# Two-level Strassen-Winograd products: the vector engine's sums in pieces between PSUM readings, the attention products ahead of long products, and q turned at the head of the stage

## The chip, the cores and the metric

The kernel runs on one core of one Trainium2 chip. The metric is the device time of one execution in microseconds. The kernel before was timed three times: 1026.94, 1013.04 and 1013.72 us, median 1013.72 us. The trace below is of a further execution, which took 1017.5 us.

## The reference

All data are float32 (the two weight matrices reach the kernel as 64-bit words, which it folds into float32 first).

```
kv  = einsum('bhsd,bhse->bhde', k, v)          # 8 batches, 8 heads, 576 x 64
o   = einsum('bhsd,bhde->bhse', q, kv)
x   = o / sqrt(mean(o*o, -1) + 1e-6) * g_norm  # then (4608, 512)
h   = x @ w_in                                 # 512 -> 2048
g   = s * max(h, 0)**2 + b
out = g @ w_out                                # 2048 -> 512
```

## The kernel before, in words

The 4608 rows are cut into 36 chunks of 128, and four chunks make a unit: nine units, u = 0 to 8. A unit has two stages. The first is x @ w_in with relu and square, by one level of the Strassen-Winograd scheme (seven products instead of eight, paid for with additions): for each of four blocks `s` of the hidden width the steps x1, z2, x6, y7, x5, x3, y4. It leaves g in SBUF as tiles a11, a12, a21, a22 and their sum s1. The second stage is g @ w_out, again by seven products. In units 2 to 8 the products 2, 7 and 4 use the scheme a second time, on quarters: `second_level` (L677) gives for each of them, called p2, p7 and p4 here, a step `sums` and seven small products in the order 1, 2, 6, 7, 5, 3, 4. Each small product is four 128x128x128 matrix products on TensorE, which the trace shows as eight MATMULs. A long product (x1, x6, x5, x3 for j = 0 and 1) has eight 128x128x256 ones, sixteen MATMULs.

`sums` makes four tiles of 128x512 on VectorE: s1 = x21 + x22 (needed by small product 5), s2 = s1 - x11 (product 6), s3 = x11 - x21 (product 7), s4 = x12 - s2 (product 3). Small products 1, 6, 5 and 3 accumulate into the same PSUM bank, and between them VectorE must read the bank: `keep` (L697 and on) takes product 1 out as r1 before product 6 may add to it, takes r2 out before product 5, and r4 before product 3. Product 2 has a bank of its own, and 7 and 4 share one. So TensorE can run ahead of a reading by only one small product.

Also on VectorE, in the second stage: the sums S2 (`s2`, four subtractions in place on a11, used by x6) and S4 (`s4`, four on a12, used by x3); and the work for the next unit's attention, chunk c = 0 to 3 of it. For each chunk `turn` transposes q in 32x32 blocks (VectorE, L391), `product` multiplies with kv on TensorE (L421, 32 MATMULs of 128 columns) into one single bank, ScalarE squares it (L430), VectorE reduces (L432), ScalarE takes the root (L436), VectorE inverts and scales (L438, L440, which frees the bank), and `turn_x` transposes the result (L464); after every second chunk ScalarE multiplies by g_norm (L470). `x_sums` (L484) then forms the four sums of the next x.

The order is written by hand: every engine runs its instructions in the order in which the program text issues them. `mm2(u)` (L646) returns 14 slots, and `side_of(u)` (L1039) gives the attention steps that follow slot n. The loop at the end runs slot, then side. Between slot 0 and slot 1 stand the last two steps (x3, y4) of the first stage. `pump(2)` lets SyncE (SP) issue the loads of the next two blocks of w_out into a ring of seven; `loads(u)` issues the q loads at the start of a unit.

In the second stage before, p2's `sums` and the reading of x1(1) come first, then all of S2, then p2's small products; S4 stands ahead of p7's small products in the same way; turn c+1 follows one slot after product c; and an attention product follows a long product.

Of the kernel before, what the change touches and what calls it, by code (L numbers as in the profile page):

```python
# [15 lines left out]
def kernel(  # L16
# [211 lines left out]
    def add(o, a, b):  # L228
        nc.vector.tensor_tensor(out=o, in0=a, in1=b, op=ALU.add)  # L229

    def sub(o, a, b):
        nc.vector.tensor_tensor(out=o, in0=a, in1=b, op=ALU.subtract)  # L232
# [410 lines left out]
    out_18 = out.rearrange("(b t j) n -> b j t n", t=32, j=JC)  # L643
    G_OF = {1: "a11", 2: "a12", 3: "a12", 4: "a22", 5: "s1", 6: "a11", 7: "a21"}

    def mm2(u):  # L646
        st = {}

        def product(i, j, ps, first):
# [27 lines left out]
        def second_level(i, other, to):  # L677


            a, t, r = {}, {}, {}  # L680
            cols = [slice(q * P, q * P + P) for q in range(2)]

            def quarter(j, h):
                g = g_pair[G_OF[i], h].rearrange("p s b t -> p (s b) t")
                return g[:, :, j * P : j * P + P]

            def sums():
                x11, x12, x21, x22 = (quarter(j, h) for j in range(2) for h in range(2))
                s1, s2, s3, s4 = (
                    late["sub"].tile([P, FC // 4, P], FP32, name="sub", tag="sub")  # L690
                    for _ in range(4)
                )
                add(s1, x21, x22)
                sub(s2, s1, x11)
                sub(s3, x11, x21)
                sub(s4, x12, s2)
                a.update({1: x11, 2: x12, 3: s4, 4: x22, 5: s1, 6: s2, 7: s3})  # L697

            def go(m, bank, first):
                if first:  # L700
                    t[bank] = bank_of((bank, i), "z" if bank == "z" else "y", 1 if bank == "z" else 2)
                    t[bank] = t[bank].rearrange("p b n -> p (b n)")[:, :P]
                n = ORDER.index(m)
                w = ring[u, i, n // 2][:, n % 2]
                for f in range(FC // 4):
                    matmul(t[bank], a[m][:, f], w[:, f], first and f == 0, f == FC // 4 - 1)

            def keep(name, j, q):
                r[name] = late["tmp"].tile([P, P], FP32, name="r", tag="r")
                scaled(r[name], t["x"], other(j, cols[q]))  # L710

            def m1():
                go(1, "x", True)
                keep("r1", 0, 0)

            def m2():
                go(2, "z", True)
                scaled(to(0, cols[0]), t["z"], r["r1"])

            def m6():  # L720
                go(6, "x", False)
                keep("r2", 1, 0)

            def m7():
                go(7, "y", True)

            def m5():
                go(5, "x", False)
                keep("r4", 1, 1)
                scaled(to(1, cols[1]), t["y"], r["r4"])  # L730

            def m3():
                go(3, "x", False)
                scaled(to(0, cols[1]), t["x"], other(0, cols[1]))

            def m4():
                go(4, "y", False)
                scaled(to(1, cols[0]), t["y"], r["r2"])

            return {"sums": sums, 1: m1, 2: m2, 6: m6, 7: m7, 5: m5, 3: m3, 4: m4}  # L740
# [26 lines left out]
        def x1(j):  # L767
            st["x", j] = half(("x", j), "x")
            product(1, j, st["x", j], True)
            if u > 0:  # L770
                part("r1", j, st["x", j], b1)
# [20 lines left out]
            else:  # L792
                scaled(rows("o1", j)[:, :HN], ps, st["r1", j])

        def s2():
            for s in range(NS):
                sub(ga["a11", s], ga["s1", s], ga["a11", s])

        def s4():
            for s in range(NS):  # L800
                sub(ga["a12", s], ga["a12", s], ga["a11", s])

        def x6(j):
# [31 lines left out]
        def seq(fn, *more):  # L835
            def run():
                fn()
                for m in more:
                    m()
            return run  # L840
# [52 lines left out]
        def x6_of(j):  # L893
            product(6, j, st["x", j], False)
            part("r2", j, st["x", j], b_12)
# [16 lines left out]
            else:  # L912
                store("o2", j, 4 * u + 2 + j)

        def run(steps, *which):
            for m in which:
                steps[m]()

        return [
            lambda: x1(0),  # L920
            seq(p2["sums"], lambda: x1(1), lambda: pump(2), s2),
            seq(lambda: run(p2, 1, 2, 6, 7), lambda: pump(2)),
            seq(p2[5], lambda: x6_of(0)),
            seq(lambda: run(p2, 3, 4), lambda: pump(2), p7["sums"]),
            seq(lambda: x6_of(1), lambda: pump(2), s4),
            seq(lambda: run(p7, 1, 2, 6, 7), lambda: pump(2)),
            seq(p7[5], lambda: x5_of(0)),
            seq(p7[3], lambda: with_7(0), p7[4], lambda: pump(2)),
            seq(lambda: x5_of(1), lambda: with_7(1), lambda: pump(2), p4["sums"]),
            lambda: x3(0),  # L930
            seq(lambda: run(p4, 1, 2, 6, 7, 5), lambda: pump(2)),
            seq(lambda: x3(1), lambda: pump(2)),
            seq(lambda: y4_of(0, 3), lambda: y4_of(1, 4), lambda: pump(2)),
        ]


    NU = FC // 2
# [101 lines left out]
    def side_of(u):  # L1039

        if u + 1 >= U:
            return {}
        turn, product, norm, turn_x, _ = zip(*(attention(c) for c in range(4 * u + 4, 4 * u + 8)))
        product = [whole(*steps) for steps in zip(product, norm)]
        side = {
            2: [turn[0]],
            3: [product[0]],
            4: [turn[1]],
            5: [turn_x[0], product[1]],
            6: [turn[2]],  # L1050
            7: [turn_x[1], product[2]],
            8: [turn[3]],
            9: [turn_x[2], product[3]],
            11: [turn_x[3]],
            12: [lambda: [sums() for sums in x_sums(u + 1)]],
        }
        if u == 0:
            side = {
                6: [lambda: kv_product(1)],
                7: [turn[0]],  # L1060
                8: [product[0], turn[1]],
                9: [turn_x[0], product[1], turn[2]],
                10: [turn_x[1], product[2], turn[3]],
                11: [turn_x[2], product[3]],
                12: [turn_x[3], lambda: [sums() for sums in sums_w_in(0)]],
                13: side[12],
            }
        return side
# [24 lines left out]
    for u in range(U):  # L1093
        if u > 0:
            loads(u)
        steps = [mm1(u, s) for s in range(NS)] if u > 0 else []
        slots = []
        for s, a in enumerate(steps):
            slots.append(a["x1"])
            if s:  # L1100
                slots.append(steps[s - 1]["x3"])
            slots.append(a["z2"])
            if s:
                slots.append(steps[s - 1]["y4"])
            slots += [a["x6"], a["y7"], a["x5"]]
        if u == 0:
            first_unit()
        for n, slot in enumerate(slots):
            slot()
            if u == 1 and n in (1, 3, 5):  # L1110
                for sums in sums_w_in((n + 1) // 2):
                    sums()
            if u in kv_due and n == 12:
                kv_product(kv_due[u])
            elif u + 1 in kv_due and n == 14:
                for i in range(2):
                    load_kv(kv_due[u + 1], i, late["kv"], tag="kv")
        second, side = mm2(u), side_of(u)
        for n, slot in enumerate(second):
            slot()  # L1120
            if u == 0:
                if n == 1:
                    for i in range(2):
                        load_kv(1, i, convp, tag="raw", bufs=3)
                    store_w2(1)
                    loads(0)
                    store_w2(5)
                elif n == 2:
                    t2 = convp.tile([P, 4 * R * D], FP32, name="w_t2", tag="raw", bufs=3)
                    W2_AT[6] = t2[:, : FC // 2 * HN].rearrange("p (f n) -> p f n", n=HN)  # L1130
                    for i in range(14, 16):
                        more(i)
                    sub_w_out(6, 3, 5)
                    store_w2(3, 2, 6)
            if n == 0 and u > 0:
                for step in ("x3", "y4"):
                    steps[-1][step]()
            for step in side.get(n, []):
                step()
        if u == 0:  # L1140
            tc_late()
            for i in range(2):
                load_kv(kv_due[1], i, late["kv"], tag="kv")
            pump(7)
# [30 lines left out]
```

## Time and profile before

| | us |
|---|---|
| the profiled execution, its own time | 1017.5 |
| its span, first to last instruction | 1015.7 |
| TensorE (PE) busy | 959.4 |
| VectorE (DVE) busy | 580.0 |
| ScalarE (ACT) busy | 194.8 |
| mean granted TensorE clock | 0.987 |
| unit 3, first stage (358.30 to 405.65 us of the span) | 47.35 |
| unit 3, second stage (405.65 to 467.56) | 61.91 |

The engine table says that TensorE is busy nearly throughout. So the view to read is that of TensorE's idle time and of who ended it, and then the order of time of TensorE and VectorE through one second stage. A row of the view in order of time has the start, the length, the engine, the line, the instruction with what it writes and reads, and how often it stands in a row; in brackets is the idle time before it and who released it. Time is in microseconds from the start of the span.

### The profile page before, as it was taken

Reading aid. Unit: us, or ns where it says so; the run is one execution under the profiler, and the core shown is the slowest. Engines: PE = TensorE matmul, PEld = TensorE weight load, DVE = VectorE, ACT = ScalarE, POOL = GpSimd, SP = SyncE. Lnnn points to the kernel's source line nnn. Section 1 sums busy time; section 2 is a strip of 40 time slices with the busy share of each in tenths; the row PEclk is TensorE's granted clock in tenths of the full one; section 3 lists DMA queues with packets and bytes.
Section 4 is the critical chain, followed back from the end, with each engine's and each line's share of the span. In section 5 each row is a group of like instructions: output and inputs, shape, how many; then the busy total and the mean of one; then the engine's idle time right before and its main releaser. Section 6 shows DMA issues by size and latency. Waiting matters only on the chain. (4 is left out here: it accounts for less than half of the span.)

```text
span 1015.7 us, 16743 instructions
## 1 busy us (share of the span) xinstructions
PE 959.4 (94%) x6934; PEld 847.5 (83%) x6934; DVE 580.0 (57%) x1019; ACT 194.8 (19%) x366; POOL 6.7 (1%) x18
## 2 busy tenths in 40 slices
PE   7999999999997999889988999799988998899987
PEld 7888888888886988779877888688877988798877
DVE  2798775564456544674465644654457455564553
ACT  3672122111210112011201121012201110112100
POOL 2000000000000000000000000000000000000000
PEclk9999999999999999999999999999999999999999
DMA  9689646687345454356164634546025522452053
GB/s 251 218 291 255 209 113 200 143 271 216 57 110 159 135 147 104 95 175 171 26 159 135 196 72 104 160 126 162 14 85 184 168 32 65 133 164 65 16 181 93
DMA packets 127531, 143.71 MB, mean 141 GB/s; under 512 B 76256, under 2 KB 87264, under 8 KB 127328
## 3 DMA queue, kind: packets, MB, share of 16 engines
q1 hardware_dynamic: 124352, 140.88, 48.6%
q10 hardware_dynamic: 2784, 1.77, 0.8%
q8 instruction: 54, 0.88, 0.4%
q14 instruction: 21, 0.17, 0.1%
q0 software_dynamic: 320, 0.00, 0.0%
HBM read 120.33 MB, written 22.28 MB: 140 GB/s over the span
## 5 line engine op out<-in xcount | busy, mean ns | idle before, releaser
L90 PE MATMUL x_ps<-w_sb,a 128*128 128x256 f32 x768 | 175.1, 382 | 0.0
L90 PEld LDWEIGHTS x_ps<-w_sb,a 128*128 128x128 f32 x768 | 144.5, 191 | 20.1 <-issue 1.6
L90 PE MATMUL y_ps<-w_sb,sub 128*128 128x128 f32 x672 | 95.6, 302 | 36.7 <-DVE r L659 36.7
L90 PEld LDWEIGHTS y_ps<-w_sb,sub 128*128 128x128 f32 x672 | 89.2, 213 | 42.5 <-DVE r L659 39.3
L90 PE MATMUL y_ps<-xs,wb 128*128 128x256 f32 x512 | 121.0, 379 | 0.0
L90 PE MATMUL x_ps<-xs,ws 128*128 128x256 f32 x512 | 121.0, 379 | 0.0
L229 DVE TENSOR_TENSOR a<-y_ps,r 128x512 f32<-128x512 f32 x64 | 44.0, 688 | 122.2 <-ACT r L568 122.2
L568 ACT COPY r<-x_ps 128x512 f32<-128x512 f32 x96 | 56.3, 586 | 284.2 <-PE x_ps L90 277.5
L90 PEld LDWEIGHTS x_ps<-xs,ws 128*128 128x128 f32 x512 | 97.3, 190 | 13.2
L90 PEld LDWEIGHTS y_ps<-xs,wb 128*128 128x128 f32 x512 | 97.3, 190 | 13.2
L90 PE MATMUL x_ps<-xT,wa 128*128 128x256 f32 x384 | 89.6, 380 | 0.1
L90 PEld LDWEIGHTS x_ps<-xT,wa 128*128 128x128 f32 x384 | 72.4, 190 | 10.2 <-ACT xT L470 0.5
L523 DVE SCALAR_TENSOR_TENSOR a<-a 128x512 f32<-128x512 f32 x96 | 66.5, 692 | 3.3
L601 DVE TENSOR_TENSOR a<-a 128x512 f32<-128x512 f32 x32 | 22.1, 692 | 75.9 <-ACT a L600 75.9
L90 PE MATMUL y_ps<-w_sb,a 128*128 128x128 f32 (+1 forms) x416 | 62.8, 297 | 0.0
L90 PE MATMUL x_ps<-xT,ws 128*128 128x256 f32 x256 | 61.1, 382 | 0.0
L90 PEld LDWEIGHTS y_ps<-w_sb,a 128*128 128x128 f32 x416 | 57.1, 191 | 4.1 <-issue 1.4
L90 PE MATMUL z_ps<-xT,wa 128*128 128x256 f32 x256 | 60.5, 379 | 0.0
L430 ACT ACTIVATE xn<-x_ps 128x512 f32<-128x512 f32 x34 | 20.3, 597 | 204.3 <-PE x_ps L421 202.9
L90 PE MATMUL x_ps<-w_sb,s 128*128 128x256 f32 x256 | 57.8, 380 | 0.0
L90 PEld LDWEIGHTS z_ps<-xT,wa 128*128 128x128 f32 x256 | 48.7, 190 | 6.6
L90 PEld LDWEIGHTS x_ps<-xT,ws 128*128 128x128 f32 x256 | 48.2, 190 | 6.7
(122 smaller groups left out, 990.3 us busy)
## 6 DMA issues: line engine op xcount, KB each, us to landing
w_sb<-w SPq DMA_DIRECT2D x133, 512.0 KB, 4.4
kv_sb<-in_k_dram SPq DMA_DIRECT2D x30, 288.0 KB, 4.8
kv_sb<-in_v_dram SPq DMA_DIRECT2D x30, 288.0 KB, 7.1
w_raw<-in_moe_w_in_dram SPq DMA_DIRECT2D x8, 1024.0 KB, 7.8
w_raw<-in_moe_w_out_dram SPq DMA_DIRECT2D x8, 1024.0 KB, 5.2
out_dram<-o SPq DMA_DIRECT2D x104, 64.0 KB, 1.7
w_sb<-w SPq DMA_DIRECT2D x21, 256.0 KB, 2.8
q_sb<-in_q_dram SPq DMA_DIRECT2D x144, 32.0 KB, 2.1
```

What stands on the lines that cost most here:

```text
L90: nc.tensor.matmul(o, lhsT=lhsT, rhs=rhs, start=start, stop=stop, skip_group_check=True)
L229: nc.vector.tensor_tensor(out=o, in0=a, in1=b, op=ALU.add)
L430: nc.scalar.activation(st["xn"], st["x"], AF.Square)
L523: nc.vector.scalar_tensor_tensor(t, t, 0.0, t, ALU.max, ALU.mult)
L568: nc.scalar.copy(st[name], src)
L601: nc.vector.tensor_mul(t, t, t)
```

## The change

Units 2 to 8 get a second stage that is written out as one sequence, `first` and `second`, in place of the 14 slots. Four things move; no instruction is added or taken away on any engine.

- `sums` takes a list. p2's s1 and s2 are made ahead of the reading of x1(1), s3 and s4 each between two readings of p2's small products. p7's and p4's sums stay whole, and stand ahead of x6(0) and x3(0).
- S2 is made in two pieces, after small product 6 and after small product 5 of p2; S4 in four pieces among p7's small products.
- turn 0 and turn 1 stand at the head of the stage, ahead of x1(0); turn 2 and turn 3 after the attention steps 1 and 2.
- An attention product with its norm (`attend`) now stands ahead of the long products x6(0), x6(1), x5(0), x5(1), and `x_sums` ahead of x3(1).

The last unit has no attention for a next one, and so only the first two. Units 0 and 1 are as before.

```diff
-            def sums():
+            def sums(which=(5, 6, 7, 3)):
...
+                for m in which:
+                    a[m] = late["sub"].tile([P, FC // 4, P], FP32, name="sub", tag="sub")
...
-        def s2():
-            for s in range(NS):
+        def s2(steps=range(NS)):
+            for s in steps:
...
-            seq(p2["sums"], lambda: x1(1), lambda: pump(2), s2),
-            seq(lambda: run(p2, 1, 2, 6, 7), lambda: pump(2)),
-            seq(p2[5], lambda: x6_of(0)),
-            seq(lambda: run(p2, 3, 4), lambda: pump(2), p7["sums"]),
-            seq(lambda: x6_of(1), lambda: pump(2), s4),
...
+        def first():
+            turn[0]()
+            turn[1]()
+            x1(0)
+        def second():
+            p2["sums"]((5, 6))
+            x1(1)
+            pump(2)
+            p2[1]()
+            p2["sums"]((7,))
+            p2[2]()
+            p2["sums"]((3,))
+            p2[6]()
+            s2((0, 1))
+            p2[7]()
+            p2[5]()
+            s2((2, 3))
+            pump(2)
+            attend(0)
+            p7["sums"]()
+            x6_of(0)
+            p2[3]()
+            p2[4]()
+            pump(2)
+            attend(1)
+            turn_x[0]()
+            turn[2]()
+            x6_of(1)
+            pump(2)
+            p7[1]()
+            s4((0,))
+            p7[2]()
+            p7[6]()
+            s4((1,))
+            p7[7]()
+            s4((2,))
+            p7[5]()
+            s4((3,))
+            pump(2)
+            attend(2)
+            turn_x[1]()
+            turn[3]()
+            x5_of(0)
+            p7[3]()
+            with_7(0)
+            p7[4]()
+            pump(2)
+            attend(3)
+            turn_x[2]()
+            x5_of(1)
+            with_7(1)
+            turn_x[3]()
+            pump(2)
+            p4["sums"]()
+            x3(0)
+            for m in (1, 2, 6, 7, 5):
+                p4[m]()
+            pump(2)
+            x_sums_next[0]()
+            x3(1)
```

VectorE in unit 3, from the sums of p2 on. Before (`sub` is a tile of `sums`; a11 with s1 is S2; `r` and `o1` are readings of small products; `or1` is the reading of x1(1); qT is a turn):

```order
L229 TENSOR_TENSOR sub_3002<-a12_2768,a12_2955 128x512
L232 TENSOR_TENSOR sub_3003<-sub_3002,a12_2768 128x512
L232 TENSOR_TENSOR sub_3004<-a12_2768 128x512
L232 TENSOR_TENSOR sub_3005<-a12_2955,sub_3003 128x512
L659 SCALAR_TENSOR_TENSOR or1_2986<-x_ps_3010,s_col_126,b_row_132 128x256
L232 TENSOR_TENSOR a11_2717<-s1_2754,a11_2717 128x512 x2
L232 TENSOR_TENSOR a11_2888<-s1_2941,a11_2888 128x512 x2
L659 SCALAR_TENSOR_TENSOR r_3033<-y_ps_3028,s_col_126,or1_2986 128x128
L659 SCALAR_TENSOR_TENSOR o1_3040<-z_ps_3035,s_col_126,r_3033 128x128
L659 SCALAR_TENSOR_TENSOR r_3046<-y_ps_3028,s_col_126,or1_2986 128x128
L391 STREAM_TRANSPOSE qT_3057<-q_sb_2671 128x512
```

The same place in the change:

```order
L229 TENSOR_TENSOR sub_3006<-a12_2768,a12_2955 128x512
L232 TENSOR_TENSOR sub_3008<-sub_3006,a12_2768 128x512
L660 SCALAR_TENSOR_TENSOR or1_2990<-x_ps_3010,s_col_126,b_row_132 128x256
L660 SCALAR_TENSOR_TENSOR r_3029<-y_ps_3024,s_col_126,or1_2990 128x128
L232 TENSOR_TENSOR sub_3031<-a12_2768 128x512
L660 SCALAR_TENSOR_TENSOR o1_3038<-z_ps_3033,s_col_126,r_3029 128x128
L232 TENSOR_TENSOR sub_3040<-a12_2955,sub_3008 128x512
L660 SCALAR_TENSOR_TENSOR r_3046<-y_ps_3024,s_col_126,or1_2990 128x128
L232 TENSOR_TENSOR a11_2717<-s1_2754,a11_2717 128x512 x2
L660 SCALAR_TENSOR_TENSOR r_3059<-y_ps_3024,s_col_126,or1_2990 128x128
L660 SCALAR_TENSOR_TENSOR o1_3061<-y_ps_3050,s_col_126,r_3059 128x128
L232 TENSOR_TENSOR a11_2888<-s1_2941,a11_2888 128x512 x2
```

Ahead of the first reading of a small product (r) there stood two sums and four parts of S2 that now stand behind it, one or two instructions at a time.

TensorE in unit 3, from p2's small products 6, 7 and 5 (the row x12) to p7's 6. Before (`bd_kv` marks an attention product, 128x256 a half of a long one):

```order
L90 MATMUL y_ps<-w_sb,sub 128x128 x12
L90 MATMUL x_ps<-w_sb,a_2717 128x256 x4
L90 MATMUL x_ps<-w_sb,a_2888 128x256 x4
L421 MATMUL x_ps<-bd_kv_114,qT 32x128 x16
L90 MATMUL y_ps<-w_sb,sub 128x128 x4
L90 MATMUL y_ps<-w_sb,a_2955 128x128 x4
```

In the change:

```order
L90 MATMUL y_ps<-w_sb,sub 128x128 x12
L421 MATMUL x_ps<-bd_kv_114,qT 32x128 x16
L90 MATMUL x_ps<-w_sb,a_2717 128x256 x4
L90 MATMUL x_ps<-w_sb,a_2888 128x256 x4
L90 MATMUL y_ps<-w_sb,sub 128x128 x4
L90 MATMUL y_ps<-w_sb,a_2955 128x128 x4
```

The attention product has passed the long product; the other three of the unit do the same.

VectorE in unit 3 around the second turn of q (qT) and S4. Before (or2 is the reading of x6, r the first reading of p7):

```order
L232 TENSOR_TENSOR sub_3120<-a21_2938,sub_3118 128x512
L391 STREAM_TRANSPOSE qT_3125<-q_sb_2671 128x512
L659 SCALAR_TENSOR_TENSOR or2_3075<-x_ps_3010,s_col_126,b_12_133 128x256
L232 TENSOR_TENSOR a12_2768<-a12_2768,a11_2717 128x512 x2
L232 TENSOR_TENSOR a12_2955<-a12_2955,a11_2888 128x512 x2
L464 STREAM_TRANSPOSE xT_3144<-xn_3094 128x4x128
L432 TENSOR_REDUCE ss_3165<-xn_3163 128x8
L438 RECIPROCAL inv_3169<-rms_3167 128x8
L440 TENSOR_TENSOR xn_3163<-x_ps_3146,inv_3169 128x8x4x16
L659 SCALAR_TENSOR_TENSOR r_3177<-y_ps_3172,s_col_126,b_row_132 128x128
```

In the change, from the same chunk's reduction on:

```order
L432 TENSOR_REDUCE ss_3146<-xn_3144 128x8
L438 RECIPROCAL inv_3150<-rms_3148 128x8
L440 TENSOR_TENSOR xn_3144<-x_ps_3127,inv_3150 128x8x4x16
L464 STREAM_TRANSPOSE xT_3153<-xn_3086 128x4x128
L391 STREAM_TRANSPOSE qT_3155<-q_sb_2688 128x512
L660 SCALAR_TENSOR_TENSOR or2_3111<-x_ps_3010,s_col_126,b_12_133 128x256
L660 SCALAR_TENSOR_TENSOR r_3175<-y_ps_3170,s_col_126,b_row_132 128x128
L232 TENSOR_TENSOR a12_2768<-a12_2768,a11_2717 128x512
L660 SCALAR_TENSOR_TENSOR o2_3183<-z_ps_3178,s_col_126,r_3175 128x128
L660 SCALAR_TENSOR_TENSOR r_3189<-y_ps_3170,s_col_126,b_row_132 128x128
```

The reduction chain stood between the reading of x6(1) and the first reading of p7, with S4 ahead of it; now it comes before that reading of x6(1), and S4 follows the reading of p7 piece by piece.

More of the change, by code (lines that the diff above doesn't have):

```diff
@@ L644, with mm2 @@
     G_OF = {1: "a11", 2: "a12", 3: "a12", 4: "a22", 5: "s1", 6: "a11", 7: "a21"}
-    def mm2(u):
+    def mm2(u, att=None):
         st = {}
@@ L685, in quarter @@
                 return g[:, :, j * P : j * P + P]
-            def sums():
+            def sums(which=(5, 6, 7, 3)):
                 x11, x12, x21, x22 = (quarter(j, h) for j in range(2) for h in range(2))
[L689 to L697, printed above, removed]
+                a.update({1: x11, 2: x12, 4: x22})
+                for m in which:
+                    a[m] = late["sub"].tile([P, FC // 4, P], FP32, name="sub", tag="sub")
+                    if m == 5:
+                        add(a[5], x21, x22)
+                    elif m == 6:
+                        sub(a[6], a[5], x11)
+                    elif m == 7:
+                        sub(a[7], x11, x21)
+                    else:
+                        sub(a[3], x12, a[6])
             def go(m, bank, first):
@@ L793, in z2, with s4 @@
                 scaled(rows("o1", j)[:, :HN], ps, st["r1", j])
-        def s2():
-            for s in range(NS):
+        def s2(steps=range(NS)):
+            for s in steps:
                 sub(ga["a11", s], ga["s1", s], ga["a11", s])
-        def s4():
-            for s in range(NS):
+        def s4(steps=range(NS)):
+            for s in steps:
                 sub(ga["a12", s], ga["a12", s], ga["a11", s])
@@ L913, in y4_of @@
                 store("o2", j, 4 * u + 2 + j)
[L915 to L920, printed above, removed]
-            seq(p2["sums"], lambda: x1(1), lambda: pump(2), s2),
-            seq(lambda: run(p2, 1, 2, 6, 7), lambda: pump(2)),
-            seq(p2[5], lambda: x6_of(0)),
-            seq(lambda: run(p2, 3, 4), lambda: pump(2), p7["sums"]),
-            seq(lambda: x6_of(1), lambda: pump(2), s4),
[L926 to L934, printed above, removed]
+        turn, product_q, norm, turn_x, x_sums_next = att or [[lambda: None] * 4] * 5
@@ new lines, in attend @@
+        def attend(c):
+            product_q[c]()
+            norm[c]()
+        def first():
[58 more added lines that the diff above has]
+            x3(1)
+            pump(2)
+            y4_of(0, 3)
+            y4_of(1, 4)
+            pump(2)
@@ L937 @@
+        return [first, second]
     NU = FC // 2
@@ L1041, in side_of @@
         if u + 1 >= U:
-            return {}
+            return None
         turn, product, norm, turn_x, _ = zip(*(attention(c) for c in range(4 * u + 4, 4 * u + 8)))
+        if u > 1:
+            sums = lambda: [sums() for sums in x_sums(u + 1)]
+            return turn, product, norm, turn_x, [sums]
         product = [whole(*steps) for steps in zip(product, norm)]
@@ L1117 @@
                     load_kv(kv_due[u + 1], i, late["kv"], tag="kv")
-        second, side = mm2(u), side_of(u)
+        side = side_of(u)
+        second = mm2(u, side if u > 1 else None)
+        if u > 1:
+            side = {}
         for n, slot in enumerate(second):
```

## The prediction

> **What bounds the kernel now.** I read the engine table first, then what TensorE waited for, then the busy time of one unit's two stages.
>
> ```profile
> span 1015.7 us, 16743 instructions
> PE 959.4 (94%) x6934; PEld 847.5 (83%) x6934; DVE 580.0 (57%) x1019; ACT 194.8 (19%) x366; POOL 6.7 (1%) x18
> ```
> ```profile
> PE y_ps L90 <- DVE r L659: 36.7, 14, 3.0
> PE x_ps L421 <- DVE qT L391: 6.8, 6, 1.1
> PE xT_ps L458 <- ACT w_raw L209: 1.4, 1, 1.4
> ```
> ```profile
> 358.30:405.65 47.35, 47.35 (x354) 41.65 (x353) 21.53 (x34) 9.28 (x18) 0.00 (x0) 1.00 0.54 127
> 405.65:467.56 61.91, 55.41 (x442) 49.30 (x440) 39.69 (x78) 8.19 (x18) 0.00 (x0) 1.00 0.42 133
> ```
>
> TensorE sets the time. Of its idle time two rows matter: 14 waits for a reading of a small product (two in each of units 2 to 8) and six for a turned q (units 2 to 7). In the window rows (length, then busy time of PE, PEld, DVE) unit 3's first stage has no idle TensorE, its second stage 6.5 us. So only the second stage can give anything. VectorE is busy there for 39.69 of 61.91 us: what matters is where its work stands. TensorE in that stage, in order of time:
>
> ```profile
> 416.01 1.05 PE L90 MATMUL y_ps<-w_sb,a 128*128 128x128 f32 x8
> 416.90 1.06 PE L90 MATMUL z_ps<-w_sb,a 128*128 128x128 f32 x8
> 420.90 2.95 PE L90 MATMUL y_ps<-w_sb,sub 128*128 128x128 f32 x24 [2.94 <-DVE r L659]
> ...
> 427.23 1.08 PE L421 MATMUL x_ps<-bd_kv,qT 128*32 128x128 f32 x32
> ...
> 430.13 3.62 PE L90 MATMUL x_ps<-w_sb,a 128*128 128x256 f32 x16
> 434.88 1.08 PE L421 MATMUL x_ps<-bd_kv,qT 128*32 128x128 f32 x32 [1.13 <-DVE qT L391]
> ...
> 436.88 1.06 PE L90 MATMUL z_ps<-w_sb,a 128*128 128x128 f32 x8
> 440.37 2.94 PE L90 MATMUL y_ps<-w_sb,sub 128*128 128x128 f32 x24 [2.43 <-DVE r L659]
> ```
>
> A small product takes 0.89 us (416.01 to 416.90). p2's products 1 and 2 run at once, then TensorE stands until 420.90, since product 6 adds to the bank that r1 is to be read from. What VectorE does meanwhile:
>
> ```profile
> 415.17 0.69 DVE L229 TENSOR_TENSOR sub<-a,a 128x512 f32<-128x512 f32 x1
> ...
> 417.10 0.68 DVE L232 TENSOR_TENSOR sub<-a,sub 128x512 f32<-128x512 f32 x1
> 417.70 0.48 DVE L659 SCALAR_TENSOR_TENSOR or<-x_ps,s_col,b_row 128x256 f32<-128x256 f32 x1
> 418.10 2.49 DVE L232 TENSOR_TENSOR a<-s,a 128x512 f32<-128x512 f32 x4
> 420.50 0.35 DVE L659 SCALAR_TENSOR_TENSOR r<-y_ps,s_col,or 128x128 f32<-128x128 f32 x1
> ...
> 422.10 0.35 DVE L659 SCALAR_TENSOR_TENSOR r<-y_ps,s_col,or 128x128 f32<-128x128 f32 x1 [0.81 <-PE y_ps L90]
> ...
> 423.89 0.35 DVE L659 SCALAR_TENSOR_TENSOR r<-y_ps,s_col,or 128x128 f32<-128x128 f32 x1 [0.70 <-PE y_ps L90]
> ```
>
> Product 1 was done at 416.90, but r1 starts at 420.50, behind four sums, the reading of x1(1) and four parts of S2. With TensorE ahead, a reading starts 0.31 us after its product (product 6 begins at 420.90, ends 0.89 later at 421.79, and its reading starts at 422.10). For p7 it is S4, a transpose and an attention's reduction that stand ahead of r1, and the turn of q stands behind four sums:
>
> ```profile
> 434.03 0.71 DVE L391 STREAM_TRANSPOSE qT<-q_sb 128x512 f32<-128x512 f32 x1
> ...
> 435.02 2.48 DVE L232 TENSOR_TENSOR a<-a,a 128x512 f32<-128x512 f32 x4
> 437.42 0.71 DVE L464 STREAM_TRANSPOSE xT<-xn 128x512 f32<-128x512 f32 x1
> 438.05 0.65 DVE L432 TENSOR_REDUCE ss<-xn 128x8 f32<-128x512 f32 x1
> ...
> 439.98 0.34 DVE L659 SCALAR_TENSOR_TENSOR r<-y_ps,s_col,b_row 128x128 f32<-128x128 f32 x1
> ```
>
> There is a second loss. The windows just behind the waits differ in the granted clock, the third number from the end:
>
> ```profile
> 308.38:311.80 3.42, 3.42 (x22) 3.42 (x23) 1.41 (x3) 0.00 (x0) 0.00 (x0) 0.71 0.17 67
> 879.86:883.30 3.44, 3.44 (x16) 3.44 (x17) 1.41 (x3) 0.00 (x0) 0.00 (x0) 0.51 0.13 51
> 420.90:424.30 3.40, 3.40 (x27) 3.35 (x28) 1.79 (x5) 0.00 (x0) 0.00 (x0) 1.00 0.26 69
> ```
> ```profile
> 308.38 4.20 PE L90 MATMUL y_ps<-w_sb,sub 128*128 128x128 f32 x24 [2.95 <-DVE r L659]
> ...
> 316.35 1.08 PE L421 MATMUL x_ps<-bd_kv,qT 128*32 128x128 f32 x32
> ...
> 985.20 2.94 PE L90 MATMUL y_ps<-w_sb,sub 128*128 128x128 f32 x24 [1.46 <-DVE r L659]
> ```
>
> After 7 of the 14 waits (both in units 2, 5 and 7, the first in unit 8) TensorE runs about 3.4 us at a lower clock. The same work, from behind the wait to the first attention product, takes 7.97 us in unit 2 (308.38 to 316.35) and 6.33 us in unit 3 (420.90 to 427.23): 1.64 us lost. Nowhere between 16.6 us and the last matmul do I find such a spell except behind a wait of 2.4 us or more; behind the 1.46 us wait at 985.20 the 24 matmuls take their usual 2.94 us.
>
> **The change part by part.** Every engine keeps its instructions; nothing is added. So the sum is made of waits that end and of waits that may begin.
>
> *p2.* Sums 3 and 4 and S2 go behind r1. Ahead of it stand two sums and the reading of x1(1), which waits for x1(1)'s end, about 416.0 + 0.31; it ends at about 416.8, before product 1's own result at 416.90 + 0.31 = 417.2. So r1 runs at 417.2 to 417.55, and product 6 could start at 416.01 + 2 x 0.89 = 417.79. The whole wait goes: 2.94 us in seven units, 20.6 us.
>
> Between r1 and r2 VectorE now has r1, a sum, a reading, a sum: 0.35 + 0.69 + 0.35 + 0.68 = 2.07 us at the most, by the durations above, where TensorE needs 2 x 0.89 = 1.78. So r2 starts up to 0.29 us late. Its slack: product 7 runs 0.89 us behind product 6, and r2 would be ready 0.31 + 0.35 = 0.66 after it, so 0.23 us are free. The cost lies between 0 and 0.06 us. I take 0, because back to back such instructions start 0.60 us apart (417.10 to 417.70) rather than 0.69. If instead each of the 28 hand-overs (r1 and r2, p2 and p7, seven units) found one whole sum in its way, it would be 0.69 - 0.23 = 0.46 each, 12.9 us. That is the upper bound.
>
> *p7.* S4 goes into pieces behind r1, and the reduction chain before the reading of x6(1). The wait of 2.43 us in six units and 1.46 in the last: 36.7 - 20.6 = 16.1 us by the grouped row. Behind small product 1 VectorE has r1, one part of S4 and a reading, less than p2.
>
> *q.* Turns 0 and 1 go to the head of the stage, where VectorE is idle:
>
> ```profile
> 409.31 0.48 DVE L659 SCALAR_TENSOR_TENSOR or<-x_ps,s_col,b_row 128x256 f32<-128x256 f32 x1 [1.36 <-PE x_ps L90]
> 411.66 0.69 DVE L601 TENSOR_TENSOR a<-a 128x512 f32<-128x512 f32 x1 [1.87 <-ACT a L600]
> ```
>
> Two turns of 0.71 us against 1.36 us idle make the reading of x1(0) at most 0.06 late, and 1.87 us of idle time follow. The 6.8 us of waits for qT go. Turn 3 is the next in line: it follows attention step 2's chain, priced by these rows:
>
> ```profile
> 428.38 0.60 ACT L430 ACTIVATE xn<-x_ps 128x512 f32<-128x512 f32 x1 [16.75 <-PE x_ps L421]
> 430.37 0.69 DVE L440 TENSOR_TENSOR xn<-x_ps,inv 128x512 f32<-128x512 f32 x1
> ```
>
> From the attention product's start at 427.23 to the end of the scaling, 431.06, are 3.83 us; turn_x and turn 3 make it about 5.2. Attention step 3 comes an attention product, a long product and two small ones after step 2, about 1.0 + 3.5 + 1.8 = 6.3 us. Covered by 1.1 us; the bank that step 2 frees after 3.83 us is covered too.
>
> *p4.* Its sums now follow the third chain: from attention step 3's start 3.83 + 0.7 for the transpose, but x5(1)'s reading waits for TensorE until about 4.9, and ends at 5.3; then a transpose (0.65), four sums (2.5), the readings of x3(0) and of p4's product 1 (0.45 + 0.35): 9.3 us. TensorE needs 1.0 + 2 x 3.5 + 1.8 = 9.8 us. The cover is half a microsecond, the thinnest after p2's. If it fails by as much, that is 0.5 us in six units, 3 us.
>
> *What each wait hides besides.* A bracket counts from the modelled end of the last matmul, which is 0.17 us after its successor could have started (1.06 against 0.89 at 416.90). Twenty waits: 3.4 us more.
>
> *The clock.* Seven spells of 1.64 us go with the waits that precede them: 11.5 us.
>
> [...]
>
> *Loads.* TensorE waits for no w_out block in the view of waits, and the ring is seven blocks deep as before. Of q the longest loads are unit 4's:
>
> ```profile
> 497.02 11.29 SPq L154 DMA_DIRECT2D q_sb<-in_q_dram  x24
> ...
> 516.51 0.69 DVE L523 SCALAR_TENSOR_TENSOR a<-a 128x512 f32<-128x512 f32 x1
> ```
> ```profile
> q_sb<-in_q_dram SPq DMA_DIRECT2D x144, 32.0 KB, 2.1
> ```
>
> They are issued by 508.3 and land by about 510.4; the turns would start at 517.2, where the sum at 516.51 ends. The margin is 6.8 us, so I cost it at nothing.
>
> The sum: 20.6 + 16.1 + 6.8 + 3.4 + 11.5 = 58.4 us. From the profiled execution's 1017.5 us that leaves 959.1 us. That execution lies 3.8 us above the median of the three runs, 1013.72, and these are 13.9 us apart. I read that spread as other numbers of slow spells (13.9 / 1.64 is 8.5 of 14); they have nothing to follow in the changed kernel, so the forecast for its median is the same 959.1 us. If the difference to the median is something else, it is 955.3.
>
> **The rivals.** *The slow spells stay.* They have another cause than the waits. For: a wait of 2.94 us is followed by one in unit 2 and by none in unit 3; against: all seven stand right behind a wait. The waits alone go: 1017.5 - 46.9 = 970.6 us.
>
> *VectorE's pieces make new short waits.* For: the cover is 0.23 us, less than a sum; against: the counts above. 12.9 + 3 us on top: 975.0 us, with no slow spells, since these waits are short.
>
> *The waits only move to the attention.* Its product ahead of the long one means that its chain runs beside four sums; if turn or bank came late by 1 us at each of the 24 products, 959.1 + 24 = 983.1. Against: covers of 1.1 us and more.
>
> *Slower: q blocks VectorE's queue.* A turn at the head of the stage holds every reading behind it until q has landed. For the gain of 58.4 us to be lost, TensorE would have to stand 58.4 / 6 = 9.7 us in each of units 2 to 7; with the margin of 6.8 us and the idle 1.87 us, q would have to land 18.4 us later than it does. Then the time would be 1017.5 us and above. Nothing in the profile delays the loads so.
>
> **How the numbers follow.** Forecast 0.79, slow spells stay 0.10, new short waits 0.07, moved waits 0.03, slower 0.01. Below the forecast lie 955.3 and, if switches between kinds of product cost a little less in the new order, 1 us more; above it the two rivals at 970.6 and 975.0, of which the first is inside. The range is 954 to 971 us. Faster by over 2% means below 993.4 us; about 2% is what a measurement of this kernel can tell from no change. Faster 0.97, within 2% 0.02, slower 0.01.
>
> **What would show it.** Right: in units 2 to 7 a second stage of about 55 us; no wait of TensorE for r or qT over 0.3 us; a granted clock of 1.00 behind p2 and p7; VectorE's 580 us unchanged, and the first stage still 47 us. Wrong: slow spells without a wait ahead of them (the first rival), many waits of 0.2 to 0.5 us for r (the second), waits of L421 (the third), or VectorE idle behind a q load at the head of the stage (the last).

## The result, and the profile after

The changed kernel takes 959.34 us (median of four runs, 958.49 to 960.35), against 1017.16 us for the kernel before (four runs, 1013.04 to 1026.94, one of them beside these). The ratio is 0.9419, with a 95% interval of 0.9344 to 0.9494. The profiled execution took 959.06 us for a span of 957.3; its span is 58.4 us shorter than before.

The engine table of the changed kernel, then its whole view of what TensorE waited for (engine, tile and line, who released it, total, times, longest):

```profile
span 957.3 us, 16744 instructions
PE 944.8 (99%) x6934; PEld 839.6 (88%) x6934; DVE 580.6 (61%) x1019; ACT 194.5 (20%) x366; POOL 6.7 (1%) x18
```
```profile
PE xT_ps L458 <- ACT w_raw L209: 1.8, 1, 1.8
PE warm_ps L90 <- POOL ident masks.py:199: 1.4, 1, 1.4
PE kv_ps L359 <- DMA kv_sb<-in_v_dram: 1.3, 2, 0.7
PE xT_ps L458 <- DVE xn L440: 0.8, 1, 0.8
PE x_ps L421 <- DVE xn L440: 0.5, 1, 0.5
PE x_ps L90 <- DVE qT L407: 0.4, 1, 0.4
PE y_ps L90 <- DVE wb L224: 0.4, 1, 0.4
```

Both rows of 36.7 and 6.8 us are gone; what is left belongs to units 0 and 1. VectorE does what it did (580.6 us against 580.0). Unit 3's two stages and the stretches behind p2's and p7's product 2, where the waits had been (length, busy time of PE, PEld, DVE, ACT, POOL, then the granted clock and the DMA share):

```profile
349.10:396.43 47.33, 47.33 (x355) 41.61 (x354) 19.87 (x30) 9.27 (x18) 0.00 (x0) 1.00 0.54 128
396.43:451.09 54.66, 54.66 (x442) 49.66 (x440) 41.40 (x81) 8.19 (x18) 0.00 (x0) 1.00 0.49 151
...
408.57:412.00 3.43, 3.43 (x50) 3.31 (x52) 3.16 (x8) 0.00 (x0) 0.00 (x0) 1.00 0.81 259
424.14:427.60 3.46, 3.46 (x51) 3.34 (x53) 2.65 (x7) 0.00 (x0) 0.00 (x0) 1.00 0.83 262
```

The second stage has 54.66 us in place of 61.91, all of it busy, and the clock is full. TensorE and VectorE there, in order of time:

```profile
406.79 1.05 PE L90 MATMUL y_ps<-w_sb,a 128*128 128x128 f32 x8
407.68 1.06 PE L90 MATMUL z_ps<-w_sb,a 128*128 128x128 f32 x8
408.57 2.84 PE L90 MATMUL y_ps<-w_sb,sub 128*128 128x128 f32 x24
411.35 1.08 PE L421 MATMUL x_ps<-bd_kv,qT 128*32 128x128 f32 x32
412.36 3.72 PE L90 MATMUL x_ps<-w_sb,a 128*128 128x256 f32 x16
```
```profile
407.27 0.48 DVE L660 SCALAR_TENSOR_TENSOR or<-x_ps,s_col,b_row 128x256 f32<-128x256 f32 x1
407.88 0.35 DVE L660 SCALAR_TENSOR_TENSOR r<-y_ps,s_col,or 128x128 f32<-128x128 f32 x1
408.15 0.68 DVE L232 TENSOR_TENSOR sub<-a 128x512 f32<-128x512 f32 x1
408.77 0.35 DVE L660 SCALAR_TENSOR_TENSOR o<-z_ps,s_col,r 128x128 f32<-128x128 f32 x1
409.04 0.68 DVE L232 TENSOR_TENSOR sub<-a,sub 128x512 f32<-128x512 f32 x1
409.67 0.35 DVE L660 SCALAR_TENSOR_TENSOR r<-y_ps,s_col,or 128x128 f32<-128x128 f32 x1
```

r1 ends at 408.23, and product 6 starts at 408.57, right behind product 2 (0.89 us after 407.68). r2 runs from 409.67 to 410.02; product 5 can start at 408.57 + 2 x 0.89 = 410.35. So r2 has 0.33 us to spare where the prediction saw between 0 and -0.06. Two of its sizes were off. From start to start a reading takes 0.27 us of VectorE and a sum 0.62 or 0.63, 0.89 us together, so VectorE keeps step with the small products instead of falling 0.29 us behind. And a reading can start 0.20 us after its product (r1 at 407.88 after product 1, done at 407.68), not 0.31: the prediction took the 0.31 from a product 6 that had just been waited for, and such a product takes 0.10 us longer (more on this below).

### The profile page after: what moved, and what is told of

Same layout as the page of the kernel before. It is cut to its first block, busy times and chain, and to the rows that moved or that the text cites. A ratio compares the mean times of both kernels' runs of the same rounds, so it can differ in the third digit from the quotient of the medians.

```text
span 957.3 us, 16744 instructions
## 1 busy us (share of the span) xinstructions
PE 944.8 (99%) x6934; PEld 839.6 (88%) x6934; DVE 580.6 (61%) x1019; ACT 194.5 (20%) x366; POOL 6.7 (1%) x18
## 4 chain that ended last, share of the span: by engine, by line
PE 96%; DMA 2%; DVE 1%; ACT 1%; issue 0%; SPq 0%; ACTq 0%; DVEq 0%
PE x_ps L90 51%; PE y_ps L90 30%; PE z_ps L90 8%; PE x_ps L421 3%; PE kv_ps L359 2%; DMA w_raw<-in_moe_w_in_dram 1%; DMA kv_sb<-in_k_dram 1%; PE qT_ps L400 0%; DVE xn L440 0%; DVE xT L464 0%; ACT xT L470 0%; ACT w_raw L209 0%; SPq L102 0%; ACT w_raw L204 0%; DVE wb L224 0%
## 5 line engine op out<-in xcount | busy, mean ns | idle before, releaser
L90 PE MATMUL y_ps<-w_sb,sub 128*128 128x128 f32 x672 | 81.8, 275 | 0.0
L90 PEld LDWEIGHTS y_ps<-w_sb,sub 128*128 128x128 f32 x672 | 80.0, 192 | 1.1
L90 PEld LDWEIGHTS x_ps<-w_sb,s 128*128 128x128 f32 x256 | 47.4, 190 | 8.4 <-issue 2.4
```

The source lines that it names most:

```text
L90: nc.tensor.matmul(o, lhsT=lhsT, rhs=rhs, start=start, stop=stop, skip_group_check=True)
```

## The experiments

Nine kernels, each timed in three rounds beside the kernel before. The theory: TensorE waits for as long as VectorE's work ahead of a due reading (or a due turn) exceeds what the reading has to spare, and no part of the change matters otherwise; a slow spell of TensorE follows an idle time of a certain length. The main rivals: one part of the change is enough, and the spells have a cause of their own. All diffs are against the changed kernel, where nothing else is said. The kernel before was timed beside three groups of these kernels, with medians of 1017.38, 1023.62 and 1016.63 us; so from kernel to kernel the times are compared here, and not the ratios.

**p2's sums and S2 whole.**

```diff
-            p2["sums"]((5, 6))
+            p2["sums"]()
             x1(1)
             pump(2)
+            s2()
             p2[1]()
-            p2["sums"]((7,))
...
-            p2["sums"]((3,))
...
-            s2((0, 1))
...
-            s2((2, 3))
```

> The changed kernel, with p2's four sums and all of S2 put back ahead of p2's small products; S4, the attention products and the turns stay where the change put them. Lateness theory: the wait ahead of p2's product 6 comes back at about 3 us in seven units and no other wait appears, 959.3 + 7 x (2.94 + 0.17) = 981.1 us, plus 1.64 us for each slow spell of TensorE; the idle times of 3.1 us are followed by a spell about half of the time, so 3 to 5 spells, 986 to 989 us. Rival, spells have a cause other than the waits: as few as the changed kernel, 981 us. Rival, only an idle time over a whole spell length (3.4 us) calls a spell: none, 981 us. Rival, the parts can stand in for one another: under 965 us.

Measured: 991.28 us (986.18 to 992.94), ratio to before 0.9751 (0.9694 to 0.9809). What TensorE waited for; then in order of time two of the seven waits; then the clock behind three:

```profile
PE y_ps L90 <- DVE r L660: 20.6, 7, 3.0
```
```profile
414.58 4.55 PE L90 MATMUL y_ps<-w_sb,sub 128*128 128x128 f32 x24 [2.95 <-DVE r L660]
```
```profile
521.41 2.94 PE L90 MATMUL y_ps<-w_sb,sub 128*128 128x128 f32 x24 [2.95 <-DVE r L660]
```
```profile
414.58:418.00 3.42, 3.42 (x16) 3.42 (x17) 0.70 (x2) 0.00 (x0) 0.00 (x0) 0.50 0.17 67
521.41:524.80 3.39, 3.39 (x44) 3.27 (x48) 1.07 (x4) 0.00 (x0) 0.00 (x0) 1.00 0.41 94
938.80:942.20 3.40, 3.40 (x22) 3.40 (x23) 0.70 (x2) 0.00 (x0) 0.00 (x0) 0.71 0.15 59
```

The wait is back to the hundredth, 20.6 us in seven units, and nothing else. The same wait of 2.95 us is followed by half the clock in one unit and by the full clock in the next; in the traced execution four of the seven were followed by a spell. So the spells come back with these waits, which the first rival forbids, and they come behind waits shorter than their own length, which the second forbids. The median is 2 us above the 986 to 989 that I expected. The runs that were not traced lost more by the clock: (1 - mean clock) x span is 7.9 us in the traced run of 986.18 us and 14.9 in those of 991.95 and 992.94.

**S2 whole alone, and the sums whole alone.** The first has only the lines on `s2` of the diff above, the second only those on `sums`.

> The changed kernel, with S2 whole ahead of p2's small products, p2's sums in pieces. Lateness theory: 4 x 0.6 us stand ahead of a reading with about 0.5 us to spare by the trace of the changed kernel (r1 at 407.88 to 408.23, product 6 at 408.57), so a wait of 1.7 to 1.9 us in seven units, 959.3 + 7 x 2.0 = 973 us, no or hardly any slow spells. Rival, it is the sums and not S2 that hold r1: under 962 us.

> The changed kernel, with p2's four sums whole ahead of the reading of x1(1), S2 in pieces. Lateness theory: two sums more, 1.2 us, ahead of a reading with about 0.4 us to spare, TensorE stands 0.6 to 0.8 us longer in seven units: 959.3 + 7 x 0.7 = 964 us, no slow spells. Rival, S2 in pieces alone is enough: 959 to 961 us.

Measured: 971.58 us (970.96 to 971.67), ratio 0.951 (0.9442 to 0.9579), and 963.49 us (963.03 to 964.73), ratio 0.9435 (0.9378 to 0.9492). The waits, S2 whole first:

```profile
PE y_ps L90 <- DVE r L660: 12.2, 7, 1.7
```
```profile
PE y_ps L90 <- DVE r L660: 3.8, 7, 0.5
```

12.2 + 3.8 = 16.0 against 20.6 us for both: either kind of piece uses the same spare time of r1, so together they cost more than each alone. Both came within 2 us of the forecast, without spells in the second stages. S2 is the larger part of p2's wait.

**S4 whole.**

```diff
+            s4()
             p7[1]()
-            s4((0,))
...
-            s4((1,))
...
-            s4((2,))
...
-            s4((3,))
```

> The changed kernel, with all of S4 put back ahead of p7's first small product, and nothing else. Lateness theory: 2.48 us of VectorE work stand ahead of a reading that has about 0.2 us to spare, a wait of 1.9 to 2.3 us ahead of p7's product 6 in seven units, 959.3 + 16.6 = 976 us, and 1.64 us for each slow spell, 0 to 4 of them. Rival, the attention chain and not S4 made p7's wait in the kernel before: under 963 us.

Measured: 970.71 us (970.16 to 971.97), ratio 0.9555 (0.9496 to 0.9615).

```profile
PE y_ps L90 <- DVE r L660: 11.1, 7, 1.6
```

The median is 5 us below the forecast of 976. The wait is 1.61 us in six units and 1.46 in the last, not 1.9 to 2.3: the four parts of S4 put 2.40 us ahead of the reading (424.89 to 427.29), and TensorE stands 1.61 + 0.17 us, so the reading had about 0.6 us to spare and not the 0.2 that I took from the kernel before. There was no spell in the second stages.

**The attention products behind the long products.** What hangs on them (the transposes, the sums of the next x) goes back with them.

```diff
-            attend(0)
             p7["sums"]()
             x6_of(0)
+            attend(0)
...
-            attend(1)
-            turn_x[0]()
-            turn[2]()
             x6_of(1)
             pump(2)
+            turn_x[0]()
+            attend(1)
+            turn[2]()
             p7[1]()
...
```

> The changed kernel, with the attention products, their chains, the transposes behind them and the sums of the next x put back behind the long products; the pieces of the sums and the early turns stay. Lateness theory: the chain of the second attention product then stands ahead of p7's first reading; from the product's start to the end of the chain are 3.83 us, the reading adds 0.35, and TensorE has 1.0 + 1.8 us of other work, so a wait of 1.4 to 2.2 us in six units: 968 to 974 us, without slow spells, since 1.46 us was followed by none. Rival, the pieces alone are enough: 959 to 961 us. Rival, any wait of over 1 us calls a slow spell: 6 x 1.64 us more, 978 to 984 us.

Measured: 970.92 us (970.46 to 971.66), ratio 0.956 (0.951 to 0.961). The wait is 1.67 us in six units:

```profile
PE y_ps L90 <- DVE r L660: 10.0, 6, 1.7
```
```profile
425.80 0.20 DVE L438 RECIPROCAL inv<-rms 128x8 f32<-128x8 f32 x1 [0.37 <-ACT rms L436]
426.11 0.69 DVE L440 TENSOR_TENSOR xn<-x_ps,inv 128x512 f32<-128x512 f32 x1
426.72 0.70 DVE L391 STREAM_TRANSPOSE qT<-q_sb 128x512 f32<-128x512 f32 x1
427.34 0.31 DVE L660 SCALAR_TENSOR_TENSOR r<-y_ps,s_col,b_row 128x128 f32<-128x128 f32 x1
```

The chain and then turn 2, which in this kernel follows it, stand ahead of r1 of p7. The turn is 0.6 us of the 1.67; without it, in the pieces alone below, the chain makes a wait of 1.07 us in five units and 1.42 in the sixth. So p7's wait in the kernel before had two causes, S4 and the chain, and either alone makes one.

**The turns of q in their old places,** with the attention products ahead.

```diff
-            turn[0]()
-            turn[1]()
             x1(0)
...
             p2[7]()
+            turn[0]()
             p2[5]()
...
             p7["sums"]()
+            turn[1]()
...
-            turn[2]()
...
             p7[7]()
+            turn[2]()
...
-            turn[3]()
...
             p7[4]()
             pump(2)
+            turn[3]()
             attend(3)
```

> The changed kernel, with the four turns of q put back to their old places (behind p2's product 7, behind p7's sums, behind p7's product 7, behind p7's product 4); the attention products stay ahead of the long products. Lateness theory: the turn now ends after its product could start, by about 1.0 us for the first, 1.0 for the second, 0.2 for the third and 1.6 for the fourth, in six units, with 0.17 for each: 959.3 + 6 x 4.3 = 985 us, four short waits per unit, no slow spells. Rival, the early turns matter only for the second product, as in the kernel before: 959.3 + 6.8 + 1 = 967 us. Rival, idle time in sum rather than in one piece calls the slow spells: 985 us and 1.64 us for each.

Measured: 977.47 us (976.49 to 977.85), ratio 0.9622 (0.9572 to 0.9673).

```profile
PE x_ps L421 <- DVE qT L391: 15.7, 18, 1.6
```

Three waits per unit, of 0.48, 0.61 and 1.50 us in the order of time (1.62 once), not four and not 4.3 us. The forecast was too high by 7.5 us, by the lengths and not by the mechanism: 959.3 + 15.7 + 18 x 0.17 = 978.1. With the attention products ahead, the early turns are worth 18.1 us, more than twice the 6.8 us that the kernel before lost for want of them. No spell followed 18 short waits.

**The pieces alone:** attention and turns both as before the change (the last two diffs together, with p7's sums behind p2's product 4).

> The kernel before, with the pieces of p2's sums, S2 and S4 alone; attention products behind the long products and turns of q as before. Lateness theory: the wait for the second turn stays as before, 1.13 us in six units; p7's first reading still has the attention chain ahead of it but no longer S4, 1.0 to 1.7 us in six units; nothing else: 959.3 + 6 x (1.1 + 1.3 + 0.34) = 976 us, no slow spells. Rival, the costs of putting back the attention order (11.6 us) and the turns (18.1 us) add up: 989 us. Rival, the attention order and the turns matter little next to the pieces: under 965 us.

Measured: 975.95 us (975.10 to 978.41), ratio 0.9559 (0.95 to 0.9618).

```profile
PE y_ps L90 <- DVE r L660: 6.8, 6, 1.4
PE x_ps L421 <- DVE qT L391: 6.8, 6, 1.1
```

The pieces alone bring 41 of the 58 us. The other two parts, put back singly, cost 11.6 and 18.1 us, and together 16.6: early turns and early attention products depend on each other, since a product that comes sooner wants its turn sooner.

**Longer and shorter waits at one place,** for the spells. The first kernel is that with p2's sums and S2 whole, with the four sums made a second time (extra work; the same values into the same tiles). The second is that with S2 whole, with the sum s3 made ahead of x1(1)'s reading. The first diff is against the kernel with p2's sums and S2 whole, the second against the changed kernel.

```diff
             s2()
+            p2["again"]()
             p2[1]()
```
```diff
-            p2["sums"]((5, 6))
+            p2["sums"]((5, 6, 7))
...
+            s2()
             p2[1]()
-            p2["sums"]((7,))
...
-            s2((0, 1))
...
-            s2((2, 3))
```

> As the kernel with p2's sums and S2 whole ahead of p2's small products, and in addition the four sums of p2 made a second time there (the same values into the same tiles, four VectorE instructions more in each of units 2 to 8), so that the wait ahead of product 6 grows from 2.94 to about 5.4 us. Lateness theory: 959.3 + 7 x (5.4 + 0.17) = 998 us without slow spells. Theory that a spell follows when most of a 3.4 us stretch of a fixed grid was idle, so that chance decides at 2.4 to 3.1 us and no longer at 5.6: a spell behind every one of the seven waits in every run, 12 us lost by the clock, each costing 1.64 us or less where its first part still lies over the wait: 1004 to 1010 us, and runs closer together than those with waits of 2.94 us. Rival, a whole stretch must be idle: (5.6 - 3.4) / 3.4 = 0.63 of them, 4 or 5 of 7. Rival, a wait of any length is followed by a spell half of the time: 3 or 4 of 7.

> As the kernel with S2 whole ahead of p2's small products, and one sum more (s3) ahead of the reading of x1(1): the wait ahead of product 6 grows from 1.74 us (no slow spell in the second stages) by 0.6 to 2.34 us in seven units. Lateness theory: 959.3 + 7 x (2.34 + 0.17) = 976.9 us without spells. Theory that a spell follows when about two thirds of a stretch of a fixed 3.4 us grid (some 2.2 us) were idle: 2.5 us idle is between the lengths that never and that always call one, so 2 to 4 spells of 1.64 us in a run, 979 to 984 us, and different numbers in different runs. Rival, the limit lies above 2.5 us and the spells behind p7 in the kernel before came from what p2's spells left: none in any run, 977 us.

Measured: 1010.93 us (1010.04 to 1011.55), ratio 0.9897 (0.9838 to 0.9957), and 982.44 us (979.88 to 983.41), ratio 0.9627 (0.9557 to 0.9697). The long wait first, then the shorter one:

```profile
PE y_ps L90 <- DVE r L660: 38.4, 7, 5.5
```
```profile
305.70:311.19 5.49, 0.01 (x1) 0.00 (x0) 5.41 (x10) 0.00 (x0) 0.00 (x0) 0.75 0.57 183
311.19:314.60 3.41, 3.41 (x16) 3.41 (x17) 0.70 (x2) 0.00 (x0) 0.00 (x0) 0.50 0.02 5
```
```profile
PE y_ps L90 <- DVE r L660: 16.4, 7, 2.3
```
```profile
307.60 4.54 PE L90 MATMUL y_ps<-w_sb,sub 128*128 128x128 f32 x24 [2.34 <-DVE r L660]
```
```profile
413.81 2.94 PE L90 MATMUL y_ps<-w_sb,sub 128*128 128x128 f32 x24 [2.35 <-DVE r L660]
```

The first median is 0.9 us above the 1004 to 1010 that I expected, the second within its range. Every wait of 5.5 us was followed by a spell, and five of the seven spells lasted 6.8 us instead of 3.4, beginning while TensorE still stood (the clock is 0.75 within the wait). The clock cost 16 to 21 us by (1 - mean clock) x span, more than the 12 I forecast, but much of that fell on the waits: the median lies 12.0 us above 959.3 + 7 x (5.48 + 0.17) = 998.9. Of the waits of 2.34 us four of seven were followed by one. Over the traced executions:

| wait | waits | followed by a slow spell |
|---|---|---|
| up to 1.75 us (S2 whole, S4 whole, attention behind, turns old, pieces alone) | 50 | 0 |
| 2.34 us (S2 and a sum) | 7 | 4 |
| 2.43 us (before, p7) | 6 | 3 |
| 2.95 us (before, p2) | 7 | 4 |
| 2.95 us (p2 whole) | 7 | 4 |
| 5.48 us (long wait) | 7 | 7 |

## Why the prediction was right

The forecast was 959.1 us; the median is 959.34.

- *The waits.* 20.6 for p2, 16.1 for p7, 6.8 for q: all 43.5 us are gone, and putting p2's work back brings back 20.6 us. p7's share splits as said, over S4 and the attention chain, and neither can be left out.
- *What a bracket leaves out,* 0.17 us per wait: unit 3's second stage fell by 7.25 us, against 2.94 + 2.43 + 1.13 + 3 x 0.17 = 7.01. The 0.24 us more are not the switches between kinds of product that the range had allowed for: going to an attention product and coming from one costs about 0.1 us each time, eight times a unit, in both kernels (in the change at 411.14 the last MATMUL ahead of it takes 0.21 us to the next start instead of 0.11, and at 412.36 the first of the long product behind it 0.32 instead of 0.22). They are restarts, which the sum had left out. Products 6, 7 and 5 of p2 and of p7 took 2.95 and 2.94 us behind their waits (rows 420.90 and 440.37 in the prediction) and take 2.84 in the change, and so do p4's, which had been held up for 0.03 us, below what the brackets show. Here are p4's, before and in the change:

```profile
459.54 2.94 PE L90 MATMUL y_ps<-w_sb,sub 128*128 128x128 f32 x24
```
```profile
443.17 2.84 PE L90 MATMUL y_ps<-w_sb,sub 128*128 128x128 f32 x24
```

In the trace the second MATMUL behind such a stand starts 0.21 us after the first, and otherwise 0.11. That is 0.3 us a unit; for q, on the other hand, the bracket hid 0.07 us instead of 0.17, since a switch to an attention product costs some 0.1 us in any case.
- *The clock.* 11.5 us for seven spells. In the changed kernel no second stage has a spell; one stands in the opening, from 23.27 to 26.68 us of the span at a clock of 0.50, behind waits there (2.12 us of idle time in the 3.41 us ahead of it). With a longer wait ahead of it (1.8 in place of 1.4 us) it makes the opening 1.3 us longer (unit 2's x1(0) starts at 294.42 in place of 293.12). This and the 0.24 us a unit (6 x 0.24 = 1.4) cancel, so that the agreement to 0.2 us is partly luck; the mechanism is not.
- *The two medians.* I took the scatter of the kernel before for a varying number of spells, and so the sum against one execution for the median after. Seven runs of the kernel before, taken beside the kernel with p2 whole, bear that out: their times lie between 1010.91 and 1022.63, and less (1 - mean clock) x span (6.1 to 20.4 us) between 1002.2 and 1004.9. Without waits to follow, the changed kernel's runs lie within 1.9 us.
- *The rivals.* The spells did not stay (970.6 us). No short waits came (975.0), nor did they move to the attention (983.1); with the pieces in step, the reading of r2 had 0.33 us to spare. p4, the thinnest cover after it, held too: its r1 ends at 442.89, 0.28 us ahead of product 6 at 443.17, where the prediction saw half a microsecond. The old places of the turns, with their 18 waits, show that the third rival's mechanism exists, and that the early turns are what avoids it. q was never late; whether the margin of 6.8 us is what the trace says was not tried.

An idle time need not be as long as a spell (3.41 us) to be followed by one: after 15 of the 27 waits between 2.3 and 3.0 us TensorE ran at half the clock.

## What to carry to other kernels

When an engine's readings free what the critical engine needs next, ask for each reading what stands ahead of it in the queue, and put long work between the readings in pieces that keep step with the critical engine (here 0.27 us for a reading and 0.62 for a sum in the 0.89 us of a small product); the total of the work need not change. Price the parts together as well as singly, because they spend the same spare time: here S2 and the sums cost 12.2 and 3.8 us of waiting, both 20.6. And count what follows a wait, not the wait alone: a wait of 2.3 to 3 us of TensorE cost another 1.6 us about half of the time here (15 of 27).

## What the runs showed of the hardware

The trace also records when the granted clock changed. In the kernel before, the seven spells have a clock of 0.50 and last 3.413 or 3.414 us each. They start at 309.82, 330.30, 640.91, 661.39, 859.36, 879.84 and 968.59 us of the span, and so 20.48, 310.61, 20.48, 197.97, 20.48 and 88.75 us apart: 6, 91, 6, 58, 6 and 26 times 3.413 us. In the 3.41 us just ahead of each the clock was 1.00, and TensorE was idle for 1.92 to 2.81 us. The two thirds of such a stretch (some 2.2 us) that I had put into the forecast for the 2.34 us wait were too much to ask for: the spells at 309.82 and 640.91 stand behind 1.97 and 1.92 us.

By length alone the waits of these traces part like this: none of 50 up to 1.75 us was followed by a spell, 15 of 27 between 2.3 and 3.0 us were, and all seven of 5.48 us. That between these lengths the place of a wait in such stretches decides is my estimate. The numbers of spells in the last two experiments, seven of seven and four of seven, lie within what it asked for, seven and two to four.

Each kernel has one trace, so the spells of its other runs were not seen. The mean clock of the 21 runs of the kernel before that were timed beside the experiments goes from 0.977 to 0.994; that its times scatter by 12 us and more because the number of spells differs is an estimate from these clocks.
